# An fp32 P·V product in a fused attention and MoE kernel: both heads of an item as one schedule unit, and three of the planner's figures changed

## Chip, cores and metric

The kernel runs on one core of a Trainium2 chip. The metric is the device time of one execution in microseconds (us). Engines are named as the profile names them: PE is TensorE (matmuls), PEld its weight loads, DVE VectorE, ACT ScalarE, POOL GpSimd, SP the engine that issues the DMAs.

## The reference, cut to what matters

Block-causal attention of 4 batches, 8 heads, 576 positions and head size 64, followed by two dense blocks on the 2304 rows of 512:

```
scores = scale * q @ k.T          # masked where block_i < block_j, blocks of 64
attn   = exp(scores - max) / (sum + 1e-9)
x      = attn @ v                 # heads side by side: 2304 x 512
h      = max(x @ w1, x @ w2, x @ w3)      # 512 -> 768
y      = h @ w_out                        # 768 -> 512
g      = (y @ w_in2) * cos(y @ w_in2)     # 512 -> 2048
out    = g @ w_out2                       # 2048 -> 512
```

## The kernel before

**Work.** Attention is cut into 32 items: a batch, a half of the query positions (low: 5 blocks of 64, 320 queries; high: 4 blocks, 256 queries), and a pair of heads. In each batch the four low items come first, then the four high ones. For an item, `scores` makes S in PSUM (one buffer, `S`, of two banks; a low item fills it once, a high item twice, as two tiles of blocks), takes the row maximum on DVE (`stat`), the exponential on ACT into `prob` (one buffer for all items), and scales the rows by the reciprocal of the sum. `transposes` turns `prob` in groups of four 128x128 blocks on PE (`tb`, two PSUM buffers) and copies each group to `pt` (one buffer). `pv` multiplies `pt` with v into `X` in PSUM (two buffers), and the result is split into a high and a low part, `xhi` and `xlo`. The first dense block of a half (units of `moe1_units`: products of `whi`, `wlo` with `xhi`, `xlo` into `psm`, then `hm`, `hh`, `hl`) is the PE work that fills the gaps of the items that follow. The second dense block (`hstage`, `ostage`) comes after all items.

**Native items.** The first eight items (batch 0; `NATIVE = 8`) are computed in fp32 while the dense block's weights are still loaded and split (`convert`, on ACT and DVE, tiles `raw`, `t`, `whi`, `wlo`, `vhi`, `vlo`); the others use a split into two parts. In a native item q lies block-diagonally in `qnat`, and the two heads of the pair share S. In P·V the v of head e is 128 x 64 and is loaded as the stationary operand; head 0 writes partitions 0 to 63 of `X`, head 1 partitions 64 to 127. A head has one matmul for each 128 keys (j): its columns are 320, 192 and 64 in a low item (576 in all), 256, 256, 256, 192 and 64 in a high item (1024). The profile shows each fp32 matmul as two MATMUL records. Each of these matmuls was a unit of its own for the planner, head 0's recorded ahead of head 1's.

**Order.** The program isn't run in the order in which it is written. `Plan` records every operation with its dependencies and a price in ns, simulates the five engines (`forward`), ranks by a backward pass (`backward`), repeats this eight times, keeps the shortest plan, and issues the instructions in that order; each engine then works through its own list in order. Operations within `R.unit()` stay together as one. Some copies and subtractions may go to one of several engines, which the plan chooses. `spent` counts a PE operation that starts before `COLD` (30 us of planned time) twice. `price` gives the cost and the latency of an operation: an fp32 matmul 4 columns/2.4 + 13 ns, a load 600 ns of issue and 2000 ns plus its bytes over 240 bytes per ns (planned one after another on a bus).

**Memory.** `qnat` and the first `raw` buffers lie in the pool `cv_start`; the pool `wk`, which holds `hm`, `hh` and `hl`, takes its place once every operation on it is done, the scores of the eighth item (item 7, counted from 0) among them. `psm` has two banks until then, so that the third group of the dense block needs a first copy to `hm`.

Of the kernel before, what the change touches and what calls it, by code (L numbers as in the profile page):

```python
# [8 lines left out]
F32 = mybir.dt.float32  # L9
# [5 lines left out]
ALU = mybir.AluOpType  # L15
# [4 lines left out]
P = 128  # L20
NLOW, NHIGH = 320, 256
# [4 lines left out]
def f32(ap):  # L26
    return ap.bitcast(F32)
# [101 lines left out]

class Plan:  # L130
    CROSS = 150.0
    COLD = 30000.0
    EARLY = 130000.0
    WEIGHT = {"DVE": 2.5, "ACT": 1.0, "POOL": 100.0}

    def __init__(self, tc):
# [106 lines left out]
    def price(self, engine, method, outs, ins, kw):  # L243


        if engine == "SP":
            tiles = outs + ins
            return 600.0, 2000.0 + sum(v.n * v.rows * 4 for v in tiles[:1]) / 240.0, False
        n = outs[0].n
        if engine == "PE":  # L250
            late = 190.0
            if method == "transpose":
                return 109.0, late, False
            dt = ins[0].buf.dt
            if dt == F32:
                return 4 * n / 2.4 + 13, late, False
            load = ins[0].n / 1.2
            return (max(n / 2.4 + 3, 65.0) if dt == BF16 else max(n / 2.4 + 13.5, load)), late, False
        psum = any(v.buf.psum for v in outs + ins)
        if method == "tensor_reduce":  # L260
            n = ins[0].n
        spread = 120.0 * (outs[0].hi - outs[0].lo + 1 > n)
        if engine == "ACT":
            scaled = isinstance(kw.get("scale"), View)
            return (n * 0.833 + spread + (55 if psum else 100) + 95 * ("bias" in kw) + 95 * scaled
                    + 93 * ("accum_out" in kw)), 112.0, False
        if engine == "DVE":
            sb = [v for v in ins if not v.buf.psum]
            fast = method in ("tensor_copy", "tensor_scalar", "memset") and not psum
            two = method in ("tensor_tensor", "scalar_tensor_tensor") and len(sb) > 1  # L270
            if method == "reciprocal":
                return 70.0 + 5 * n, 100.0, False
            return n * (0.52 if fast else 1.04) + 68 + spread, 88.0, fast or two
        return (n * 3.3 + 75 if method == "tensor_tensor" else max(400.0, n * 1.04 + 195)), 45.0, method != "memset"
# [5 lines left out]
    def after(self, d, o, stop):  # L280
        if d.engine == "PE" and o.engine == "PE":
            return -d.late
        if d.engine == "CTL" or o.engine == "CTL":
            return 0.0
        return self.CROSS if stop > self.EARLY else 35.0

    def spent(self, o, start):
        return o.cost * (2 if o.engine == "PE" and start < self.COLD else 1)

    def forward(self, rank):  # L290
# [15 lines left out]
        def release(o):  # L306
# [5 lines left out]
            if o.ways:  # L312
                def done(way):
                    e, (cost, late, shared), _ = way
                    start = max(free[e] + load[e], at)
                    if shared:
                        start = max(start, port)
                    return start + cost * self.WEIGHT[e] + late
                chosen[o] = min(o.ways, key=done)
# [121 lines left out]
def fused_kernel(tc, qk, v2, w1, w2, w3, wout, w_in2, w_out2, out):  # L441
# [11 lines left out]
    R = Plan(tc)  # L453
# [7 lines left out]
    at = R.open(name="at", bufs=1, side="right")  # L461
    ps_x = R.open(name="ps_x", bufs=1, space=PSUM, side="right")
# [49 lines left out]
    for u in range(2):  # L512
        f = Half()
# [15 lines left out]
    for b in range(B):  # L529
        for half in range(2):  # L530
            for pair in range(HP):
                it = Item()
# [54 lines left out]
    def scores(it):  # L587
# [4 lines left out]
        for tile_ in f.tiles:  # L592
# [15 lines left out]
            for b, b0, c0, n, c in tile_:  # L608
                i = b - f.first
                part = s[:, :, c0:c0 + n] if c == 2 else s[:, b0, c0:c0 + n]  # L610
                R.vector.tensor_reduce(st[:, i:i + 1], part, axis=AX.XY if c == 2 else AX.X, op=ALU.max, negate=True)
                bias = st[:, i:i + 1]
# [32 lines left out]
    def pv(it):  # L645
        f = it.f
        n = f.n
        h, l = xhi[it.half][:, it.pair], xlo[it.half][:, it.pair]
        where = {}
        for c, (j, b) in enumerate(f.order):  # L650
            where.setdefault(j, []).append((c, b))
        if it.native:
            X = ps_x.tile([P, 512], F32, "X", tag="X", bufs=2)
        else:
            x32 = at.tile([P, NLOW], F32, "x32", tag="x32")
        for e in range(2):
            a, o = 64 * e, 64 - 64 * e
            if not it.native:
                X = ps_x.tile([P, 512], F32, "X", tag="X", bufs=2)
            for j in range(f.nj):  # L660
                c0, b0 = where[j][0]
                nb = len(where[j])
                q0 = 64 * (b0 - f.first)
                if not it.native and q0 >= f.both:

                    v = it.vs[:, j, 2 * e:2 * e + 2].rearrange("p a d -> p (a d)")
                    dst = X[:, f.both:2 * n - f.both].then(
                        lambda ap, q=q0 - f.both: ap.rearrange("p (c q) -> p c q", c=2)[:, :, q:])
                    dst.n = 2 * (n - q0)
                    R.tensor.matmul(dst, v, it.pt[:, :, c0:c0 + nb, a:a + 64], start=j == 0, stop=j == f.nj - 1,  # L670
                                    skip_group_check=True)
                    continue
                with R.unit():
                    for i in range(1 if it.native else 2):
                        p = it.pt[:, i, c0:c0 + nb, a:a + 64]
                        if it.native:
                            R.tensor.matmul(X[a:a + 64, q0:n], it.vr[:, j, e], p, start=j == 0,
                                            stop=j == f.nj - 1, skip_group_check=True)
                        else:
                            v = it.vs[:, j, 2 * e:2 * e + 2].rearrange("p a d -> p (a d)")  # L680
                            R.tensor.matmul(X[:, q0:n], v, p, start=j == 0 and i == 0, stop=j == f.nj - 1 and i == 1,
                                            skip_group_check=True)
            if not it.native:
                R.scalar.copy(x32[a:a + 64, :n], X[o:o + 64, :n])
                R.vector.tensor_tensor(x32[a:a + 64, :n], X[a:a + 64, :n], x32[a:a + 64, :n], ALU.add).cost += 118.0
                R.vector.tensor_tensor(x32[a:a + 64, f.both:n], X[a:a + 64, n:2 * n - f.both], x32[a:a + 64, f.both:n],
                                       ALU.add).cost += 118.0
        if it.native:
            R.copy(h, X[:, :n])
            R.vector.tensor_tensor(l, X[:, :n], f32(h), ALU.subtract)  # L690
        else:
            R.copy(h, x32[:, :n])
            R.sub(l, x32[:, :n], f32(h))


    bank_pools = [(ps_m, 2)]
# [106 lines left out]
    for n in range(NI + 1):  # L803
        conv = CONV.get(n, (0, 0, 0))
        if n:
            transposes(items[n - 1])
        for step in range(3):
            if step == 1 and n < NI:
                scores(items[n])
                if n + LA < NI:  # L810
                    load(items[n + LA])
            if step == 2 and n:
                it = items[n - 1]
                pv(it)
                if it.pair == HP - 1:
                    if it.n == HP - 1:
                        R.close(cv_start)
                        wk = R.open(cv_start, name="wk", bufs=1)
                    fill += zip([*range(1, 3 * NFF + 1)] + NK * [4 * NFF], moe1_units(it.b, it.half))
            for _ in range(conv[step]):  # L820
                conv_next()
            units((0.3, 0.35, 0.35)[step])
        if n + 1 < NI:
            prep(items[n + 1])
        if n > 9 and n % 3:
            ahead()
# [174 lines left out]
```

## Time and profile before

| | |
|---|---|
| median of 3 runs | 929.67 us (929.02 to 930.89) |
| profiled execution | 929.6 us, span 927.5 us |
| PE busy | 899.2 us, 97% of the span, 5388 matmuls |
| PEld busy | 801.7 us, 86% |
| DVE busy | 662.7 us, 71% |
| ACT busy | 478.7 us, 52% |
| mean granted TensorE clock | 0.994 of full speed |

The span goes from the first to the last instruction; the time of the execution has some 2 us around it. Busy shares are means over stages that differ: a table by stretches is needed to see where an engine sits idle. Every instruction is recorded by one helper (L208), so groups are told apart by tiles: `X<-pt,vr` is the fp32 P·V product, `X<-pt,vs` that of the later items.

### The profile page before, as it was taken

Reading aid. Unit: us, or ns where it says so; the run is one execution under the profiler, and the core shown is the slowest. Engines: PE = TensorE matmul, PEld = TensorE weight load, DVE = VectorE, ACT = ScalarE, POOL = GpSimd, SP = SyncE. Lnnn points to the kernel's source line nnn. Section 1 sums busy time; section 2 is a strip of 40 time slices with the busy share of each in tenths; the row PEclk is TensorE's granted clock in tenths of the full one; section 3 lists DMA queues with packets and bytes.
Section 4 is the critical chain, followed back from the end, with each engine's and each line's share of the span. In section 5 each row is a group of like instructions: output and inputs, shape, how many; then the busy total and the mean of one; then the engine's idle time right before and its main releaser. Section 6 shows DMA issues by size and latency. Waiting matters only on the chain.

```text
span 927.5 us, 14314 instructions
## 1 busy us (share of the span) xinstructions
PE 899.2 (97%) x5388; PEld 801.7 (86%) x5388; DVE 662.7 (71%) x1402; ACT 478.7 (52%) x1080; POOL 0.7 (0%) x7
## 2 busy tenths in 40 slices
PE   6888999999999999999999999999999999999998
PEld 5656989999999999999999988888888888888897
DVE  6979868999889887677776899855555555455554
ACT  5867457776767765766664553442224223322233
POOL 0000000000000000000000000000000000000000
PEclk9899999999999999999999999999999999999999
DMA  7455332442443421212003592220001000100010
GB/s 218 151 156 170 116 136 92 149 160 95 135 138 113 144 66 39 64 34 89 15 1 123 179 370 96 58 78 14 1 1 69 0 1 1 46 1 0 1 46 23
DMA packets 39492, 78.51 MB, mean 85 GB/s; under 512 B 9728, under 2 KB 20992, under 8 KB 39424
## 3 DMA queue, kind: packets, MB, share of 16 engines
q1 hardware_dynamic: 39424, 77.61, 25.3%
q8 instruction: 42, 0.69, 0.3%
q14 instruction: 26, 0.21, 0.1%
HBM read 61.34 MB, written 16.25 MB: 84 GB/s over the span
## 4 chain that ended last, share of the span: by engine, by line
PE 84%; DVE 9%; ACT 4%; issue 1%; DMA 1%; ACTq 0%; DVEq 0%; SPq 0%
PE psm L208 48%; PE po L208 21%; PE S L208 8%; ACT prob L208 4%; PE tb L208 3%; DVE stat L208 3%; PE X L208 3%; DVE t L208 2%; DVE x L208 1%; DVE pt L208 1%; DVE qbd L208 0%; DVE hm L208 0%; DMA qk<-qk 0%; DVE vs L208 0%; DVE wlo L208 0%
## 5 line engine op out<-in xcount | busy, mean ns | idle before, releaser
L208 PE MATMUL psm<-yh,w_in 128*128 128x512 f32 (+1 forms) x640 | 193.3, 368 | 0.0
L208 PE MATMUL psm<-xhi,whi 128*128 128x320 f32 (+1 forms) x576 | 177.3, 308 | 3.1 <-DVE hm L208 2.3
L208 PE MATMUL po<-w_out,gh 128*128 128x512 f32 x576 | 177.7, 390 | 0.0
L208 PE MATMUL psm<-xhi,wlo 128*128 128x320 f32 (+1 forms) x576 | 170.4, 296 | 0.0
L208 PE MATMUL psm<-xlo,whi 128*128 128x320 f32 (+1 forms) x576 | 170.2, 296 | 0.0
L208 ACT ACTIVATE th<-th,halfpi 128x512 f32<-128x512 f32 (+1 forms) x80 | 54.4, 682 | 187.9 <-DVE th L208 187.8
L208 PEld LDWEIGHTS psm<-yh,w_in 128*128 128x128 f32 x640 | 117.1, 188 | 20.5
L208 PEld LDWEIGHTS po<-w_out,gh 128*128 128x128 f32 x576 | 107.1, 188 | 21.4
L208 PE MATMUL psm<-yl,w_in 128*128 128x512 f32 (+1 forms) x320 | 117.7, 368 | 0.0
L208 PEld LDWEIGHTS psm<-xhi,whi 128*128 128x128 f32 x576 | 109.3, 190 | 6.2 <-DVE hm L208 4.5
L208 PE MATMUL po<-w_out,gl 128*128 128x512 f32 x288 | 112.0, 389 | 0.0
L208 PEld LDWEIGHTS psm<-xlo,whi 128*128 128x128 f32 x576 | 109.3, 190 | 0.1
L208 PEld LDWEIGHTS psm<-xhi,wlo 128*128 128x128 f32 x576 | 109.0, 189 | 0.0
L208 ACT ACTIVATE prob<-S,stat 128x128 f32<-128x128 f32 (+8 forms) x144 | 74.8, 526 | 55.2 <-DVE stat L208 50.7
L208 DVE TENSOR_SCALAR th<-psm 128x512 int32<-128x512 f32 (+1 forms) x80 | 50.8, 637 | 69.0 <-PE psm L208 69.0
L208 DVE TENSOR_REDUCE stat<-S 128x1 f32<-128x320 f32 (+8 forms) x144 | 64.8, 484 | 48.4 <-PE S L208 34.8
L208 DVE TENSOR_TENSOR th<-psm,th 128x512 f32<-128x512 f32 (+1 forms) x80 | 50.9, 637 | 51.6 <-ACT th L208 51.5
L208 DVE TENSOR_TENSOR gl<-th,gh 128x512 fp32r<-128x512 f32 (+1 forms) x80 | 50.8, 636 | 35.0 <-ACT gh L208 34.7
L208 PEld LDWEIGHTS psm<-yl,w_in 128*128 128x128 f32 x320 | 60.3, 188 | 10.7
L208 ACT CAST gh<-th 128x512 fp32r<-128x512 f32 (+1 forms) x76 | 43.7, 575 | 49.9 <-DVE th L208 49.4
L208 PEld LDWEIGHTS po<-w_out,gl 128*128 128x128 f32 x288 | 54.0, 188 | 11.3
L208 PE MATMUL tb<-ident,prob 128*128 128x128 f32 x400 | 60.2, 277 | 2.0 <-ACT pt L208 0.8
(87 smaller groups left out, 1520.8 us busy)
## 6 DMA issues: line engine op xcount, KB each, us to landing
raw<-w SPq DMA_DIRECT2D x18, 512.0 KB, 3.9
raw<-w_in SPq DMA_DIRECT2D x16, 512.0 KB, 3.6
raw<-w_out SPq DMA_DIRECT2D x16, 512.0 KB, 3.6
vr<-v SPq DMA_DIRECT2D x16, 320.0 KB, 3.3
qk<-qk SPq DMA_DIRECT2D x12, 416.0 KB, 3.3
kept_in<-both SPq DMA_DIRECT2D x9, 512.0 KB, 2.6
w_in<-kept_in SPq DMA_DIRECT2D x9, 512.0 KB, 9.6
out<-osb SPq DMA_DIRECT2D x18, 256.0 KB, 2.0
```

Of the source, the lines that this page charges most:

```text
L208: return lambda: getattr(real, method)(*[value(a) for a in args], **{k: value(a) for k, a in kw.items()})
```

## The change

The P·V product of a native item becomes one unit: for each j the matmul of head 0 and then that of head 1, all 6 (low) or 10 (high) without anything between, and `SWITCH` (295 ns) is added to the unit's price. The price of an fp32 matmul with 64 output rows is halved. A load is priced at 330 bytes per ns instead of 240. `COLD` is 0: no PE operation counts twice. The rest of `pv`, that of the later items, is the same work with other indentation. No computed value changes.

```diff
-    COLD = 30000.0
+    COLD = 0.0
     EARLY = 130000.0
+    SWITCH = 295.0
...
-            return 600.0, 2000.0 + sum(v.n * v.rows * 4 for v in tiles[:1]) / 240.0, False
+            return 600.0, 2000.0 + sum(v.n * v.rows * 4 for v in tiles[:1]) / 330.0, False
...
             if dt == F32:
-                return 4 * n / 2.4 + 13, late, False
+                return (4 * n / 2.4 + 13) / (2 if outs[0].rows == 64 else 1), late, False
...
         if it.native:
+
             X = ps_x.tile([P, 512], F32, "X", tag="X", bufs=2)
-        else:
-            x32 = at.tile([P, NLOW], F32, "x32", tag="x32")
+            with R.unit():
+                for j in range(f.nj):
+                    c0, b0 = where[j][0]
+                    q0 = 64 * (b0 - f.first)
+                    for e in range(2):
+                        a = 64 * e
+                        p = it.pt[:, 0, c0:c0 + len(where[j]), a:a + 64]
+                        R.tensor.matmul(X[a:a + 64, q0:n], it.vr[:, j, e], p, start=j == 0, stop=j == f.nj - 1,
+                                        skip_group_check=True)
+                R.unit_op.cost += R.SWITCH
+            R.copy(h, X[:, :n])
+            R.vector.tensor_tensor(l, X[:, :n], f32(h), ALU.subtract)
+            return
...
                 with R.unit():
-                    for i in range(1 if it.native else 2):
+                    for i in range(2):
                         p = it.pt[:, i, c0:c0 + nb, a:a + 64]
-                        if it.native:
-                            R.tensor.matmul(X[a:a + 64, q0:n], it.vr[:, j, e], p, start=j == 0,
-                                            stop=j == f.nj - 1, skip_group_check=True)
```

## Rows read from the trace of the kernel before

**Rows 1.** The page's first part: busy us, share of the span, instructions of each engine.

```profile
PE 899.2 (97%) x5388; PEld 801.7 (86%) x5388; DVE 662.7 (71%) x1402; ACT 478.7 (52%) x1080; POOL 0.7 (0%) x7
```

**Rows 2.** Busy time by stretches: us, then PE, PEld, DVE, ACT, POOL; PEclk.

```profile
0.00:84.00 84.00, 64.87 (x328) 45.07 (x330) 68.55 (x191) 58.63 (x148) 0.73 (x7) 0.94 0.56 173
84.00:121.00 37.00, 36.83 (x255) 35.68 (x255) 31.82 (x70) 19.78 (x39) 0.00 (x0) 1.00 0.38 126
127.00:500.00 373.00, 368.02 (x2699) 357.73 (x2700) 297.59 (x681) 250.18 (x635) 0.00 (x0) 1.00 0.28 92
```

**Rows 3.** Timeline, 76 to 93 us, all engines: start us, us, engine, operation.

```profile
82.16 1.77 PE L208 MATMUL S<-qk,qnat 128*128 128x512 f32 x4 [0.57 <-ACT prob L208]
...
83.97 0.43 ACT L208 COPY hm<-psm 128x320 f32<-128x320 f32 x1 [0.31 <-PE S L208]
...
84.45 0.41 PE L208 MATMUL psm<-xhi,whi 128*128 128x320 f32 x1
```

**Rows 4.** Timeline of PE, 53 to 63 us: an item of the high half.

```profile
55.15 0.65 PE L208 MATMUL X<-pt,vr 128*64 128x256 f32 x2
55.73 0.66 PE L208 MATMUL tb<-ident,prob 128*128 128x128 f32 x4
56.31 1.08 PE L208 MATMUL X<-pt,vr 128*64 128x256 f32 x8
57.97 1.77 PE L208 MATMUL S<-qk,qnat 128*128 128x512 f32 x4 [0.57 <-ACT prob L208]
59.67 1.08 PE L208 MATMUL X<-pt,vr 128*64 128x256 f32 x10
```

**Rows 5.** Timeline of PE, 86 to 93 us: two X records between psm.

```profile
91.88 0.31 PE L208 MATMUL psm<-xhi,wlo 128*128 128x320 f32 x1
92.12 0.54 PE L208 MATMUL X<-pt,vr 128*64 128x192 f32 x2
92.59 0.41 PE L208 MATMUL psm<-xhi,whi 128*128 128x320 f32 x1
```

**Rows 6.** Timeline, 33 to 50.4 us, all engines: two low items.

```profile
37.52 1.21 PE L208 MATMUL X<-pt,vr 128*64 128x320 f32 x12
...
45.02 1.08 PE L208 MATMUL X<-pt,vr 128*64 128x320 f32 x4
...
45.39 0.20 ACT L208 ACTIVATION_READ_ACCUMULATOR prob<-S,stat 128x1 f32 x1
...
46.02 1.77 PE L208 MATMUL S<-qk,qnat 128*128 128x512 f32 x4
```

**Rows 7.** Chain that ended last, 60 to 130 us: start us, us, what.

```profile
68.20 0.58 PE X L208 x2
68.78 0.60 PE tb L208 x4
```

**Rows 8.** Timeline of PE, 112 to 130 us: the last native item.

```profile
121.42 1.08 PE L208 MATMUL X<-pt,vr 128*64 128x256 f32 x4
...
123.50 2.44 PE L208 MATMUL X<-pt,vr 128*64 128x256 f32 x16
126.37 0.42 PE L208 MATMUL psm<-hh,vhi 128*128 128x320 f32 x1 [0.44 <-ACT vhi L208]
```

**Rows 9.** Chain that ended last, 0 to 60 us: DVE between two scores.

```profile
19.64 0.33 DVE whi L208
...
25.05 0.60 DVE t L208
```

**Rows 10.** Timeline, 48 to 76 us: first score tile of two high items.

```profile
50.48 1.99 PE L208 MATMUL S<-qk,qnat 128*128 128x288 f32 x8 [1.56 <-ACT prob L208]
...
62.75 3.68 PE L208 MATMUL S<-qk,qnat 128*128 128x288 f32 x8 [2.00 <-ACT prob L208]
```

**Rows 11.** Busy time by stretches, 64 to 66 us; the granted clock is PEclk.

```profile
64.00:66.00 2.00, 2.00 (x7) 1.61 (x6) 0.84 (x3) 1.11 (x3) 0.00 (x0) 0.50 0.68 229
```

**Rows 12.** DMA issues: KB each, median us from issue to landing.

```profile
raw<-w SPq DMA_DIRECT2D x18, 512.0 KB, 3.9
```

More of the change, by code (lines that the diff above doesn't have):

```diff
@@ L653, in pv @@
             X = ps_x.tile([P, 512], F32, "X", tag="X", bufs=2)
-        else:
-            x32 = at.tile([P, NLOW], F32, "x32", tag="x32")
+            with R.unit():
[11 more added lines that the diff above has]
+            return
+        x32 = at.tile([P, NLOW], F32, "x32", tag="x32")
         for e in range(2):
             a, o = 64 * e, 64 - 64 * e
-            if not it.native:
-                X = ps_x.tile([P, 512], F32, "X", tag="X", bufs=2)
+            X = ps_x.tile([P, 512], F32, "X", tag="X", bufs=2)
             for j in range(f.nj):
@@ L663, in pv @@
                 q0 = 64 * (b0 - f.first)
-                if not it.native and q0 >= f.both:
-                    v = it.vs[:, j, 2 * e:2 * e + 2].rearrange("p a d -> p (a d)")
+                v = it.vs[:, j, 2 * e:2 * e + 2].rearrange("p a d -> p (a d)")
+                if q0 >= f.both:
                     dst = X[:, f.both:2 * n - f.both].then(
@@ L673, in pv @@
                 with R.unit():
-                    for i in range(1 if it.native else 2):
+                    for i in range(2):
                         p = it.pt[:, i, c0:c0 + nb, a:a + 64]
-                        if it.native:
-                            R.tensor.matmul(X[a:a + 64, q0:n], it.vr[:, j, e], p, start=j == 0,
-                                            stop=j == f.nj - 1, skip_group_check=True)
[L679 to L693, printed above, removed]
+                        R.tensor.matmul(X[:, q0:n], v, p, start=j == 0 and i == 0, stop=j == f.nj - 1 and i == 1,
+                                        skip_group_check=True)
+            R.scalar.copy(x32[a:a + 64, :n], X[o:o + 64, :n])
+            R.vector.tensor_tensor(x32[a:a + 64, :n], X[a:a + 64, :n], x32[a:a + 64, :n], ALU.add).cost += 118.0
+            R.vector.tensor_tensor(x32[a:a + 64, f.both:n], X[a:a + 64, n:2 * n - f.both], x32[a:a + 64, f.both:n],
+                                   ALU.add).cost += 118.0
+        R.copy(h, x32[:, :n])
+        R.sub(l, x32[:, :n], f32(h))
     bank_pools = [(ps_m, 2)]
```

## Prediction

> **What bounds the kernel now.** I read the page's busy shares first: PE is busy 97% of the span [rows 1], so the time falls only where PE has less to do, or where it sits idle on the way. The table by stretches says where that is [rows 2]: up to 84 us PE is busy 64.87 of 84.00 us, so 19.1 us are idle; from 84 to 121 us 0.2 us are idle, from 127 to 500 us 5.0 of 373. The native items run up to about 121 us, nearly all their scores before 84. So there are two regimes: a first one that ends when a chain of scores, maximum, exponential and transposes has gone through the items, and a second one in which PE's own work sets the end.
>
> The timeline shows what divides them [rows 3]: the first copy to `hm` at 83.97 us waited for the last score tile of item 7 (issued at 82.16), since `hm` lies where `qnat` was; the third group of the dense block starts at 84.45, when that copy has freed a bank. From there PE is dense. Hence the arithmetic of this prediction: the end moves by as much as item 7's last score tile moves, and by as much as PE's work behind it changes. P·V work ahead of it that merely fills a wait is worth nothing.
>
> **What P·V costs now.** Two X records of 256 columns hold PE for 0.58 us until the next instruction, two of 192 columns for 0.47 [rows 4, 5]: 0.11 us for 64 columns, 1.7 ns each, and 0.15 us besides. Ahead of the latter the last psm starts 0.24 us earlier, where psm go at 0.145 us a piece (36.83 us for 255) [rows 2, 5]: another 0.1 us to get in. So an excursion to X costs 0.25 us beyond its columns. One head at a time, a high item would need 1024 x 1.7 ns = 1.7 us twice; heads in turn, once. That they do run at once is in the trace: a low item's 12 records, 576 columns for each head, took 1.21 us, where the columns of both one after the other make 1.9 us [rows 6]; and in a high item 8 records (four matmuls of 256 columns, 0.43 us each) took 1.08 us where 1.7 would be due [rows 4]. So the planner already put some heads side by side; it didn't in the last item. A whole high unit comes to 1.7 + 0.25 = 1.95 us, a low one to 0.96 + 0.25 = 1.2.
>
> **Part by part.**
>
> *The split transposes.* In a high item the first X matmul sits between the third and the fourth group of tb: 55.15 to 55.73 us [rows 4]. The chain of waits carries it as a piece of its own, 0.58 us at 68.20, with tb on both sides [rows 7]: the exponential of the next item waits for the last tb, because `prob` is one buffer, and the next score tile waits for that exponential. The unit needs all of `pt`, so it can't stand there. Items 4, 5 and 6 have the pattern: 3 x 0.58 = 1.7 us. Bounds: 0, if the fourth tb then waits for its PSUM buffer as long, and 1.7.
>
> *Item 3.* The exponential that frees S ends at about 45.5 us (45.39 + 0.20, overlapping); the score tile starts at 46.02, after an X of 45.02 to 46.02 [rows 6]. As `pt` isn't whole then, the unit must go behind: 0.5 us. Bounds 0 and 0.5.
>
> *The rest of the X work of items 0 to 5* stands ahead of waits: X ends near 57.4 and the score tile begins at 57.97, and the one from 59.67 is followed by a wait of 2.00 us [rows 4, 10]. I cost its shortening at nothing: it only lengthens waits for the exponential. That cover also hides the unit, 1.95 us from about 59.1 (after the score tile, as `pt` is whole only then), since PE has nothing due before 62. A wrong position could put all 1.95 us on the chain of an item.
>
> *Item 6.* X went 83.86 to 84.45 inside the wait for `hm`, and in two later excursions of which one cost 0.56 us (0.71 from psm to psm, less 0.15) and the other, of 64 columns, 0.2 less. The unit starts at the same place and takes 1.95 us instead of 0.59: +1.36 - 0.56 - 0.36 = +0.4 us. Bounds: -0.9, if the unit fits in ahead, and +1.4.
>
> *Item 7.* Two excursions among dense psm: 121.42 to 122.43, 1.0 us, and 123.50 to 126.37, 2.87 us with 0.44 of waiting for `vhi` at the end [rows 8]. The unit takes 1.95: 3.88 - 0.44 - 1.95 = 1.5 us less. Bounds: 0, if the wait for `vhi` grows by all of it, and 1.9. I take 1.5: DVE has 5.2 idle us from 84 to 121 [rows 2], in which a conversion can come earlier.
>
> *The consumers.* A unit issues no DMA. `xhi` of a native item now comes after the whole unit; the next item's copies to `pt`, and on SP the v load for two items on, wait for its last matmul, with the raw weight loads queued behind that one. With the unit ending some 0.3 us after the present X (59.1 + 1.95 against 59.67 + 1.08), nobody is late.
>
> *The planner's figures* remove no work; they change order. Load price: 512 KB come to 4.2 us by 240 and 3.6 us by 330, and the trace shows 3.9 [rows 12], between both. `COLD`: PE's clock was granted in full for most of the first 30 us. What a better order may give is in the chain between the score tiles of 13.5 and 26.4 us: ten pieces of weight conversion on DVE, ahead of the maximum, from 19.64 to 25.65 us, 4.9 us in sum [rows 9]. The same is the price of a worse order, since nothing forbids such a pile at another item. I take 0, with -4.9 and +4.9 for the range.
>
> Sum: -1.7 - 0.5 + 0.4 - 1.5 = -3.3 us. The profiled execution took 929.6 us, the median of the runs is 929.67: the same. Forecast 926.3 us. What this measurement can tell from no change is about 0.2%, 1.9 us.
>
> **Rivals.**
>
> *Conversions set the end of the first regime (within 0.2%).* If the dense block starts 2.2 us earlier while `vhi` and `vlo` keep their dates, PE waits for them instead of at the scores. For it: the wait at 126.37 us [rows 8]. Against it: DVE's 5.2 idle us. Then item 7's term is lost too and only some 0.6 us remain: 929.0. Chance 0.22.
>
> *The clock falls more often (slower).* In the trace PE sits idle 2.00 us, and the score tile behind runs 3.68 us where the same one took 1.99 after an idle 1.56 [rows 10]; the granted clock there is 0.50, that is 1.2 GHz instead of 2.4 [rows 11]. That costs 1.7 us on the chain. The unit takes some 1.5 us of PE work out of each high item and empties the stretch between tb and the second score tile (56.3 to 57.4) [rows 4]. Two more such tiles eat the gain; with four the time is 926.3 + 4 x 1.7 = 933.1. Against it: the later and longer unit fills part of the gap that now has the fall. Chance 0.13. The Trainium skill has this as a rule ("TensorE: Matmul & The Clock Gate", section "HAM oscillation — how this bites in real kernels"): waits between bursts of matmuls send the array back to half rate; by it a change that thins PE's work in a stretch with waits is to be feared. The trace agrees that a fall followed a wait, and shows waits after which none came.
>
> *A worse order early (slower).* Conversions pile up ahead of a maximum at one more item: 926.3 + 4.9 = 931.2, somewhat more with a cold tile behind it. Chance 0.09.
>
> *A better order early.* The ten pieces leave the chain: 926.3 - 4.9 = 921.4. Chance 0.14.
>
> **How the numbers follow.** The forecast (924 to 927.8) has 0.42. The range takes in a better early order with some room for its X terms, the rival within 0.2%, and the nearer half of the slower ones: 920.5 to 932.5. Left out are four cold tiles and more (0.1) and gains over 9 us (0.07). Faster by over 0.2%: 0.42 + 0.14 = 0.56; within 0.2%: 0.22; slower: 0.13 + 0.09 = 0.22.
>
> **What would show it.** Eight X pieces, one an item, of about 1.2 us (low) and 1.95 us (high); four tb groups in a row; the first `hm` copy near 81.8 us instead of 83.97; X records in item 7 in one piece; PE's busy time lower by several us, most of which comes back as idle time ahead of the first `hm` copy. Wrong would be: PEclk of 0.5 in more stretches than now, longer waits for `vhi`, or a first `hm` copy that is no earlier, since then order, not P·V, set the first regime.

## The result, and the profile after

The changed kernel takes 921.54 us (median of 4 runs) against 930.10 for the kernel before, run beside it on the same chip: ratio 0.9911, 95% interval 0.9893 to 0.9928, 8.3 us less by the ratio. The forecast was 926.3, 3.3 us less. The sign and the range held; the size did not.

The first part of the page of the changed kernel (its profiled execution took 921.26 us), to be read beside [rows 1]:

```profile
span 919.5 us, 14322 instructions
PE 890.7 (97%) x5388; PEld 799.6 (87%) x5388; DVE 653.4 (71%) x1380; ACT 488.5 (53%) x1102; POOL 0.7 (0%) x7
```

PE issues the same 5388 matmuls and is busy 8.5 us less; the span is 8.0 us shorter. So the idle time of PE is, in sum, what it was. Where it lies is another matter. The four stretches below end at the same points of the work in both kernels: the last fp32 score tile has been issued, the first P·V product of the later items starts, the last one ends, the span ends. First the kernel before, then the changed one (columns as in [rows 2]):

```profile
0.00:83.86 83.86, 64.73 (x326) 44.93 (x326) 68.52 (x190) 58.60 (x147) 0.73 (x7) 0.94 0.56 173
83.86:144.85 60.99, 59.83 (x422) 56.79 (x422) 48.45 (x111) 34.95 (x84) 0.00 (x0) 1.00 0.37 123
144.85:495.63 350.78, 346.30 (x2529) 336.01 (x2528) 282.20 (x648) 236.72 (x599) 0.00 (x0) 1.00 0.28 90
495.63:927.50 431.87, 428.33 (x2116) 364.00 (x2114) 263.53 (x456) 148.42 (x250) 0.00 (x0) 1.00 0.17 58
```

```profile
0.00:81.36 81.36, 59.38 (x317) 43.13 (x317) 65.65 (x178) 62.09 (x158) 0.74 (x7) 0.92 0.54 172
81.36:139.28 57.92, 57.92 (x433) 56.57 (x432) 48.29 (x111) 35.88 (x85) 0.00 (x0) 1.00 0.46 155
139.28:487.65 348.37, 345.12 (x2529) 335.88 (x2528) 278.36 (x645) 238.10 (x603) 0.00 (x0) 1.00 0.27 87
487.65:919.50 431.85, 428.33 (x2116) 364.00 (x2114) 261.07 (x449) 152.39 (x257) 0.00 (x0) 1.00 0.17 58
```

The first stretch is 2.5 us shorter (forecast 2.2), the second 3.1 (forecast 1.1), the third 2.4 (forecast 0), the fourth the same. In the first, PE is busy 5.35 us less and idle 2.85 us more: the shortened P·V work mostly becomes waiting, as forecast. In the second PE has no idle time left, where it had 1.16 us. The third holds nothing that the change computes otherwise: 2529 instructions on PE both times.

The boundary between the first two, as [rows 3] showed it before, in the timeline of the changed kernel:

```profile
79.66 1.77 PE L209 MATMUL S<-qk,qnat 128*128 128x512 f32 x4 [1.86 <-ACT prob L209]
...
81.36 1.96 PE L209 MATMUL X<-pt,vr 128*64 128x256 f32 x20
...
81.60 0.44 ACT L209 COPY hm<-psm 128x320 f32<-128x320 f32 x1
...
83.24 0.41 PE L209 MATMUL psm<-xhi,whi 128*128 128x320 f32 x1
```

The copy to `hm` comes at 81.60 instead of 83.97, but PE then works through the unit of item 6 (1.88 us from start to start) and the dense block begins at 83.24, 1.2 us earlier, not 2.4. Items 4 and 7 of the changed kernel (timeline of PE), beside [rows 4] and [rows 8]:

```profile
52.61 1.27 PE L209 MATMUL tb<-ident,prob 128*128 128x128 f32 x8 [0.24 <-ACT pt L209]
55.46 1.77 PE L209 MATMUL S<-qk,qnat 128*128 128x512 f32 x4 [1.59 <-ACT prob L209]
57.16 1.96 PE L209 MATMUL X<-pt,vr 128*64 128x256 f32 x20
59.91 1.99 PE L209 MATMUL S<-qk,qnat 128*128 128x288 f32 x8 [0.80 <-ACT prob L209]
```

```profile
118.58 1.96 PE L209 MATMUL X<-pt,vr 128*64 128x256 f32 x20
120.47 0.42 PE L209 MATMUL psm<-hh,vhi 128*128 128x320 f32 x1
```

X is one piece in each item: 1.96 us by its record and 1.89 until the next instruction in a high item at full clock, 1.20 and 1.13 in a low one. No X stands between the tb groups.

### The profile page after: what moved, and what is told of

Its sections match the earlier page's. It is cut to its first block, busy times and chain, and to the rows that moved or that the text cites. A ratio compares the mean times of both kernels' runs of the same rounds, so it can differ in the third digit from the quotient of the medians.

```text
span 919.5 us, 14322 instructions
## 1 busy us (share of the span) xinstructions
PE 890.7 (97%) x5388; PEld 799.6 (87%) x5388; DVE 653.4 (71%) x1380; ACT 488.5 (53%) x1102; POOL 0.7 (0%) x7
## 4 chain that ended last, share of the span: by engine, by line
PE 88%; DVE 6%; ACT 4%; issue 1%; DMA 0%; POOLq 0%; ACTq 0%; POOL 0%; DVEq 0%; SPq 0%
PE psm L209 51%; PE po L209 21%; PE S L209 8%; PE X L209 4%; PE tb L209 4%; ACT prob L209 3%; DVE stat L209 2%; DVE t L209 1%; DVE pt L209 1%; DVE x L209 1%; DMA raw<-w 0%; DVE wlo L209 0%; DVE hm L209 0%; DVE prob L209 0%; DVE vs L209 0%
## 5 line engine op out<-in xcount | busy, mean ns | idle before, releaser
L209 ACT ACTIVATE prob<-S,stat 128x320 f32<-128x320 f32 (+8 forms) x144 | 74.8, 527 | 47.9 <-DVE stat L209 43.7
```

Source lines behind the costliest of these rows:

```text
L209: return lambda: getattr(real, method)(*[value(a) for a in args], **{k: value(a) for k, a in kw.items()})
```

## The experiments

Each ratio is to the kernel before, run beside it on the same chip. The experiments ask two things: what heads in turn are worth when nothing else moves, and what a new order is worth when nothing else changes.

### The parts of the change

`unit_only` is the unit without the two general figures, `figures_only` those figures without the unit; `unit_cold` and `unit_load` have the unit and one figure each.

```diff
# unit_only: from the changed kernel; unit_cold keeps the first, unit_load the second
-    COLD = 0.0
+    COLD = 30000.0
-  ... sum(v.n * v.rows * 4 for v in tiles[:1]) / 330.0, False
+  ... sum(v.n * v.rows * 4 for v in tiles[:1]) / 240.0, False
# figures_only: the same two lines the other way, in the kernel before
```

> The changed kernel with COLD back at 30000 and the load price back at 240, so that of the change only the unit is left (heads in turn, halved price, SWITCH). P.V theory (the gain is PE time of the product, 8.6 us under the kernel before for the whole change): nearly all of it, -6 to -8 us, about 923. Order theory (the surplus over the forecast -3.3 came from the planner's two figures): about -3.3 us, 926.8. Draw theory (each new plan shifts the time by some us, whatever the reason): anything from 920 to 930, and no sum over the parts.

> The kernel before with COLD 0 and the load price 330, P.V as it was. P.V theory: within 1.5 us of before, 929 to 931. Order theory: -3 to -6 us, 924 to 927, the middle and later stretches shorter. Draw theory: anything from 926 to 934.

> The unit and COLD 0, load price 240. Order theory (COLD is what brought the rest): like the changed kernel, 921 to 923. Draw theory: the stretch of the native items as in the changed kernel (last fp32 score tile at 81 us, first later P.V at 139 to 140.5), the stretch of the later items anything from 348 to 353 us: 921.5 to 927.5.

> The unit and the load price 330, COLD 30000. Order theory (the load price brought the rest): like the changed kernel, 921 to 923. Draw theory: native stretch as in the changed kernel, the later one from 348 to 353 us: 921.5 to 927.5.

Measured: unit_only 0.9978 (0.9968 to 0.9987), figures_only 0.9995 (0.9986 to 1.0004), unit_cold 1.0003 (0.9993 to 1.0013), unit_load 0.9991 (0.9977 to 1.0004). No part is near 0.9911. The unit gives -2.1 us, the figures -0.5, the unit with either figure -0.8 or +0.3, and all three -8.3: the parts don't add up. That speaks against both the theory that the product's PE time is the whole gain and the theory that one figure brought the surplus. unit_only (927.2 us) came out near the 926.8 of the order theory; unit_cold (930.1) and unit_load (928.8) are slower than every range given for them, the draw theory's 921.5 to 927.5 too. No run has the unit without its own two prices (`SWITCH` and the halved matmul price), so what is called the unit here is always the three together.

### Heads one after the other, in the same plan

`heads_after` changes only the order of the matmuls within the unit; its price and its place in the plan are those of the changed kernel. `heads_late` does it in items 0 to 5 alone.

```diff
 # heads_after
-                for j in range(f.nj):
...
-                    for e in range(2):
+                for e in range(2):
+                    for j in range(f.nj):
 # heads_late
+                turns = [(j, e) for j in range(f.nj) for e in range(2)]
+                if it.n < 6:
+                    turns.sort(key=lambda je: je[1])
+                for j, e in turns:
```

> The changed kernel with the matmuls of the unit in another order: all of head 0, then all of head 1; prices, and so the plan, stay the same. P.V theory: a high unit goes from 1.9 to about 3.1 us and a low one from 1.2 to about 1.8; the 4 x 1.2 + 4 x 0.6 = 7 us of PE time are on the chain only where the unit stands before work that is due (item 3 in turn before transposes, item 6 and item 7 in dense matmuls): +2.5 to +4 us, 924 to 925.5. If alternation did nothing: 0. Order theory: the plan holds, so no more than +2.5 us as well.

> The changed kernel, same plan, heads in turn in items 6 and 7 alone; items 0 to 5 run head 0 and then head 1 within the unit. The run with the heads one after the other in all items was 6 us slower than the changed kernel: 3.2 us by the last fp32 score tile (one more stretch at half clock among them), 3.0 between it and the first P.V of the later items. If what is worth something is PE time after that tile (P.V theory with the two regimes): this kernel keeps the 3.0 and loses at most 3.2, 922 to 924.5. If the units ahead of the tile are hidden by waits, as the prediction had it: 0 to +1 us, about 922.

Measured: heads_after 0.9977 (0.9969 to 0.9986), 6 us above the changed kernel and so above the +4 that was expected at most; heads_late 0.9947 (0.9929 to 0.9965), between the two, and with a median of 925.0 us above both of its ranges. In the three traces PE goes through the same groups of matmuls in the same order, so the plan is indeed the same. The timeline of PE in heads_late:

```profile
58.08 3.30 PE L209 MATMUL X<-pt,vr 128*64 128x256 f32 x20
61.31 1.99 PE L209 MATMUL S<-qk,qnat 128*128 128x288 f32 x8
...
81.61 3.36 PE L209 MATMUL S<-qk,qnat 128*128 128x512 f32 x4 [1.87 <-ACT prob L209]
84.90 1.96 PE L209 MATMUL X<-pt,vr 128*64 128x256 f32 x20
```

With one head after the other a high unit takes 3.23 us until the next instruction, and the score tile behind it starts without a wait: the unit is too long for the gap, where in turn it left 0.80 us of it unused. That, the same in other items, and a stretch at half clock (the score tile at 81.61 takes 3.36 us instead of 1.77) put the start of item 6's product at 84.90 instead of 81.36: 1.95 us of this have come together by the start of the last score tile (81.61 against 79.66), and that tile at half clock adds 1.59. The table by stretches of heads_late, and its second stretch in heads_after:

```profile
84.90:142.82 57.92, 57.92 (x433) 56.58 (x433) 48.30 (x111) 35.71 (x84) 0.00 (x0) 1.00 0.45 147
142.82:490.93 348.11, 344.85 (x2527) 335.63 (x2526) 278.23 (x644) 238.04 (x603) 0.00 (x0) 1.00 0.28 87
```

```profile
84.90:145.54 60.64, 60.64 (x432) 58.46 (x432) 48.64 (x111) 35.87 (x84) 0.00 (x0) 1.00 0.44 140
```

In the second stretch heads_late is equal to the changed kernel to the last digit, 57.92 us, and heads_after has 2.7 us more, from items 6 and 7 alone. The third stretch, here up to the start of the last P·V record, is 348.1 us as in the changed kernel up to the same point: it belongs to the plan, not to the product. So in one and the same plan heads in turn are worth 6 us, about 3.5 before the boundary (1.6 of them by the tile at half clock) and 2.7 behind it. The kernel before had part of that already, since its planner had put some heads side by side.

### A nuisance in the plan

Four kernels draw a new order and do nothing else: `CROSS`, an assumed latency between engines late in the plan, 5 ns up or down, with and without the change. Two more shift the load price by 3%.

```diff
# cross_155, cross_145: the changed kernel; before_cross_155, before_cross_145: the kernel before
-    CROSS = 150.0
+    CROSS = 155.0        # or 145.0
# load_320, load_340: the changed kernel
-  ... / 330.0, False
+  ... / 320.0, False     # or 340.0
```

> The changed kernel with the planner's CROSS (an assumed latency between engines late in the plan) at 155 instead of 150: a nuisance, nothing is done differently but a new order is drawn. P.V and order theory: within 1.5 us of the changed kernel. Draw theory: 2 us and more away from it, up or down.

> The kernel before with the planner's CROSS at 155 instead of 150: the nuisance without the change. Draw theory: the later items' stretch (350.6 us before) moves by 1 to 3 us either way, the native one by less than 1: 927 to 933. Order theory: within 1 us of before.

> The changed kernel with CROSS at 145 instead of 150. With 155 the native stretch stayed as it was to 0.3 us and the later items took 2.8 us more. Draw theory: the same again, native stretch to 81 us, later stretch 349 to 353: 922 to 927. If the changed kernel's order is good for a reason: 920 to 923.

> The kernel before with CROSS at 145: a third draw without the unit. Draw theory: 927 to 933. The unit's own worth is then the mean of the draws with it less the mean of those without: -3 to -4 us, against -8.6 for the one pair of this change.

> The changed kernel with a load price of 320 instead of 330. If 330 is simply the truer figure: within 1.5 us of the changed kernel, 920 to 923. Draw theory (the order of the later items comes out by chance, 348 to 353 us there, and the changed kernel had the best so far): 922 to 930, more probably 924 to 928.

> The changed kernel with a load price of 340. As for 320: 920 to 923 if the figure is what counts, 922 to 930 by the draw theory, with no relation to the result of 320.

All kernels in one table; the last columns are of the one profiled execution: start of the last fp32 score record, start of the first P·V record of the later items, and from there to the start of the last one (all from the views of the tiles S and X).

| kernel | ratio (95%) | last fp32 score | first later P·V | later items |
|---|---|---|---|---|
| before | 1 | 83.4 | 144.9 | 350.5 |
| before_cross_145 | 1.0017 (1.0005 to 1.0030) | 84.4 | 145.8 | 352.6 |
| before_cross_155 | 1.0019 (1.0010 to 1.0028) | 82.6 | 144.0 | 351.7 |
| figures_only | 0.9995 (0.9986 to 1.0004) | 84.2 | 143.2 | 353.1 |
| **changed** | **0.9911 (0.9893 to 0.9928)** | 80.9 | 139.3 | 348.1 |
| cross_145 | 0.9980 (0.9969 to 0.9990) | 81.6 | 140.0 | 352.5 |
| cross_155 | 0.9954 (0.9940 to 0.9968) | 81.2 | 139.5 | 351.0 |
| load_320 | 0.9989 (0.9977 to 1.0002) | 82.9 | 143.0 | 352.3 |
| load_340 | 0.9979 (0.9957 to 1.0000) | 80.6 | 140.2 | 352.9 |
| unit_only | 0.9978 (0.9968 to 0.9987) | 81.0 | 140.5 | 352.8 |
| unit_load | 0.9991 (0.9977 to 1.0004) | 82.6 | 140.8 | 351.2 |
| unit_cold | 1.0003 (0.9993 to 1.0013) | 81.4 | 127.1 | 367.6 |

unit_cold draws an order in which later items begin before more of the dense work; its two last columns can't be set beside the others. Of the rest, the seven kernels with the unit reach the first later P·V at 139.3 to 143.0 us, the four without it at 143.2 to 145.8: means 140.5 and 144.5, 4.0 us apart, without overlap. The stretch of the later items is 348.1 to 352.9 with the unit and 350.5 to 353.1 without: it doesn't go with the unit, and the changed kernel has the shortest of all eleven. The mean ratio is 0.9973 over the eight draws with the unit and 1.0008 over the four without: 0.35%, 3.2 us. The ratios scatter by 2.7 us (standard deviation) with the unit and by 1.1 us without, so this mean is known to about 1.1 us either way; without the changed kernel, the best of its eight, it is 2.4 us. That plans differ by several us without a reason bears out the draw theory, but its ranges were too low here too: cross_145 (928.0 us) is above 922 to 927, and load_320 (928.3) above the 924 to 928 called more probable.

How the nuisance makes its difference is seen in the waits of PE in that stretch (engine and tile, what it waited for, us in total, times, longest). The changed kernel, then cross_145:

```profile
PE S L209 <- ACT prob L209: 1.5, 2, 0.9
PE psm L209 <- DVE hm L209: 1.1, 3, 0.5
PE tb L209 <- DVE pt L209: 0.4, 2, 0.2
```

```profile
PE psm L209 <- DVE hm L209: 3.8, 7, 1.4
PE psm L209 <- ACT hm L209: 0.8, 3, 0.5
PE S L209 <- DVE stat L209: 0.8, 2, 0.4
PE S L209 <- ACT prob L209: 0.6, 1, 0.6
PE tb L209 <- DVE pt L209: 0.2, 1, 0.2
```

It is the same work with the same matmuls, and 3.0 or 6.2 us of waits: a `psm` bank comes free a little late ten times instead of three. The rest of the 4.4 us between the two is PE busy a little longer. Which step of the new order brings these waits was not traced.

## Why the prediction was wrong in size

**What P·V costs** was right: 1.89 us until the next instruction for a high unit (1.95 forecast), 1.13 for a low one (1.2), eight pieces, tb groups in a row. The two regimes and their boundary were right: heads_late shifts the boundary by 3.5 us and leaves what is behind it as it was.

**The planner's figures** is the step that failed: "I take 0, with -4.9 and +4.9 for the range". It looked for the effect of a new order only in the first 30 us. The runs show that even 5 ns in one constant redraw the order, and the later items, where the change does nothing, came out 2.4 us shorter. A change of 5 ns in one assumed latency undid that and more (cross_155 +2.9 us, cross_145 +4.4 in that stretch). As a mean over draws 0 was fair there (351.5 us with the unit, 352.0 without); as the value of this one draw it missed 2.4 of the 4.7 us by which the four stretches beat the sum.

**Item 7** was undersized. The two terms behind the boundary made -1.1 us; the stretch came out 3.1 shorter. Item 6 went as forecast: the unit starts in the same place, the dense block 1.2 us earlier after a boundary that was 2.5 earlier, so +1.3 of the +1.36 forecast, and the two later excursions, forecast at -0.9, are gone. Item 7 took 1.89 us. What was left out: I had kept the waits for `vhi`, `vlo` and `hm` (1.16 us in all), and none is left; and some 0.9 us more are gone, most of it from psm records, of which fewer stand next to an excursion (from start to start, the psm of the second dense product take 0.7 us less). In the other plans with the unit that are comparable this stretch, first later P·V less last fp32 score, is 58.2 to 60.1 us, without it 59.0 to 61.5, by the means 58.9 and 60.8: 1.9 us for the forecast 1.1, so the 3.1 are partly a good draw.

**The split transposes and item 3** gave the right sum, -2.2 against -2.5, by other steps, which is luck. Item 3 is there: 10.34 us from the first score tile of item 4 to that of item 5 (37.51 to 47.85) against 11.01 before. But from there to the second score tile of item 7 the changed kernel needs 31.81 us and the kernel before 31.68: the -1.7 us of the transposes are not in it. The timeline of the changed kernel shows one place where they went:

```profile
63.50 1.15 PE L209 MATMUL tb<-ident,prob 128*128 128x128 f32 x8 [0.24 <-ACT pt L209]
64.79 0.67 ACT L209 ACTIVATE raw<-raw 128x512 int32<-128x512 uint32 x1 [0.85 <-DMA raw<-w]
65.36 0.73 ACT L209 ACTIVATE prob<-S,stat 128x576 f32<-128x576 f32 x1
...
66.85 2.40 PE L209 MATMUL S<-qk,qnat 128*128 128x512 f32 x4 [2.20 <-ACT prob L209]
```

The transposes are done early, but on ACT a conversion that waits for its weight load now stands ahead of the exponential, and the clock falls over the tile and the unit that follow (2.96 us for the latter). unit_only needs 39.68 us from the first score tile of item 4 to the second of item 7 (38.79 to 78.47), against 42.69 before (39.47 to 82.16). But the clock fell in this stretch before, at the tile of 3.68 us [rows 10], and not in unit_only, as the granted clock of the two stretches shows (before, then unit_only; columns as in [rows 2]):

```profile
39.47:82.16 42.69, 35.01 (x187) 23.79 (x187) 36.90 (x93) 30.45 (x70) 0.00 (x0) 0.96 0.49 155
```

```profile
38.79:78.47 39.68, 29.14 (x177) 20.02 (x177) 37.55 (x97) 30.51 (x70) 0.00 (x0) 1.00 0.53 169
```

That is 1.7 of the 3.0 us. Over all draws the same stretch takes 39.7 to 45.2 us with the unit and 41.5 to 44.1 without, by the means 42.8 and 42.7. So over the draws these two terms are not found, though the changed kernel has item 3's.

In the changed kernel the gain of the first regime comes earlier, from the low items: its first high tile is at 37.51 instead of 39.47. In the draws with the unit that tile lies between 35.4 and 38.8 us, in those without between 38.8 and 40.4. The chain that ended last shows one thing that changed: the ten pieces of conversion of [rows 9] have left it. Up to the first high tile it held 9.5 us of conversions before (tiles `t`, `whi`, `wlo`) and holds 3.3 now; between the second score tile and the third, where the ten stood, there is one piece, on ACT:

```profile
15.40 2.43 PE S L209 x10
...
21.73 0.57 ACT raw L209
...
22.63 2.90 PE S L209 x10
```

A load of `qk`, 3.9 us, has left the chain too. In their place stand longer pieces of score tiles (10.8 us instead of 7.7), exponentials (7.3 instead of 5.2) and tb and X (4.4 instead of none). Which of these steps gives the 2.0 us net, and which edit brought it, was not tried. So it is the order that moved the first regime too, by a step that the prediction had as a rival (a better order early, 921.4 us). That the measured 921.5 is next to that figure is a coincidence: the tile came 2.0 us earlier, not 4.9, and the larger part of the gain lies behind the boundary.

**The rest of the X work of items 0 to 5** was costed at nothing. heads_late speaks against that: in the changed kernel's plan, heads one after the other in these six items put the last score tile 1.95 us later. 0.5 us of it are there at the first high tile (38.00 against 37.51). How much of this the change itself had gained can't be read off, as the kernel before has another order and had some heads side by side.

**The rivals.** The clock did fall more often, four times instead of twice before the boundary, but one of the two stretches before was twice as long: in sum 13.6 us at half clock against 10.2 (the mean granted clock of the first stretch is 0.92 against 0.94). A tile wholly at half clock costs about what was said, 1.6 us (3.36 against 1.77 in heads_late). The rest of the stretch got shorter by more than that, so the sum stayed a gain. Each of the four falls comes within about a microsecond of the end of a wait of 2.1 to 3.9 us. That waits send the clock down is the rule of the Trainium skill ("TensorE: Matmul & The Clock Gate", section "HAM oscillation — how this bites in real kernels"), and the trace agrees. That less P·V work brings more falls is not borne out: over the draws the time at half clock is 6.8 to 13.7 us with the unit and 6.8 to 13.6 without, and heads_late, with more P·V work in the same plan, has 17.1. Conversions did not become the bound: the waits for `vhi` and `vlo` vanished.

So as the mean over draws the change is worth 3.2 us, give or take 1.1, where 3.3 were forecast; but as the gain ahead of the boundary was not found where the forecast had it, this agreement is in part luck. The one order that this change comes with is some 6 us better than the mean of its kind. Whether a plan like it could be had on purpose stays open: of the other seven kernels with the unit the nearest, cross_155, stays 4 us behind.

## What to carry to other kernels

Where a list scheduler lays out the whole program, an edit can redraw all of it, as 5 ns in one constant did here: before crediting an edit with its time, redraw it a few times with a nuisance constant, with and without, and compare the means. Here single draws lay between 921.5 and 930 us with the unit, so a pair of runs, however narrow its interval, measures a draw. To price the edit itself, hold the plan and change only what is issued, as with the heads here, and read it stretch by stretch between points that mean the same work.

## What the runs showed of the hardware

That two fp32 products of 64 output columns each run side by side was in the trace before. Not expected was that they overlap a little even when issued one after the other: in the kernel before, the low item at 19.41 us has its 12 records issued head by head and takes 1.79 us for them, less than the 1.9 of the columns alone, since the second head's first record starts (20.003 us) while three of the first head's are still to start (20.160, 20.322 and 20.378). heads_after, whose edit fixes the order of issue, has the same: 1.79 us for a low unit and 3.30 for a high one by the record, where the columns of the latter make 3.4. There too three records of the first head are still to start, so the overlap was seen to reach only a few records ahead; in turn the units take 1.20 and 1.96.
